# A planner's costs, its settings and its written order change in a fused attention and mixer block on one core

## Chip, core and metric

The kernel runs on one core of one Trainium2 chip. The metric is the device time of one execution in microseconds (us), the median of the runs taken. The trace comes from one profiled execution; its span runs from the first to the last instruction, and its device time is a little longer.

The engines are named as in the profile: PE is TensorE (PEld its weight loads), DVE VectorE, ACT ScalarE, POOL GpSimd, SP the queue that issues all DMAs. Each engine works through its own instructions strictly in the order in which they were put down.

## The reference, cut to what is computed

```python
# S = 2048 rows, D = 448, H = 16 heads of 28, W = 8 keys at distance 0, 2, ... 14; F = 1792
def _A_ref(x, wqkv, wo):
    q, k, v = split(x @ wqkv)
    idx = pos[:, None] - (arange(8) * 2)[None, :]          # masked where idx < 0
    logits = einsum("bhsd,bhswd->bhsw", q, k[idx]) * Dh ** -0.5
    return einsum("bhsw,bhswd->bhsd", softmax(logits), v[idx]) @ wo

def _B_ref(x, w1, w2, w3, w4):
    h = gelu(layernorm(x) @ w1)
    hs = concat(h quarters, moved by 1, -1, 2, -2 rows) @ w2
    x1 = x + hs
    return x1 + gelu(layernorm(x1) @ w3) @ w4

h  = x + _A_ref(layernorm(x), A_wqkv, A_wo)
h2 = h + _B_ref(layernorm(h), B_w1, B_w2, B_w3, B_w4)      # returned
```

## The kernel before

The 2048 rows are 16 tiles of 128 rows, handled in four blocks `t` of four tiles. The work of a block is cut into phases. `N1` normalizes the block's rows into the buffer `lntm` (mean and variance on DVE, the power -0.5 on POOL into `rs_y`, minus mean times that into `nmr`, then one pass for each tile on the engine that NORM names: `a` ACT, `v` DVE, `p` POOL). A small DVE `COPY lntm<-lntm` then repeats the last 64 columns of the block's four tiles at once. `A1` turns `lntm` into `actT` (TURN: `t` is 16 PE transposes and their eviction by ACT, `d` a DMA transpose that SP issues) and makes q, k and a joint rest `r` on PE: seven groups, whose accumulators (`ps`) ACT evicts into `arena`. `V` makes v, which ACT evicts into `vt` and DMAs spread into `vw`. `A2` makes the products of q with eight shifted k on DVE (`qk_r`, four instructions: three of 4096 columns and one of 2048), sums them on PE with a 0/1 matrix `zc`, and does the softmax (`mx`, `ls`, `zs`, `pb`), whose result PE transposes through `ident`. `A3` spreads the weights into a band on DVE (`bd_r`, a product with the mask `bmask`, four a block), multiplies with `vw` on PE, and then `wo_s` (the part `O`); the residual is added either on PE (the rows `ps<-xin,ident`) and evicted by ACT, or on DVE (RESIDUAL; PE too wherever the row sums are taken on the way). `B1` is the second normalization and `w1` (`ps<-actT,w_s`), `B2` the product with `w2` (`ps<-w_s,arena`) and the third normalization. From `B2` on the tiles form units `u` of 3, 4, 4, 4 and 1 tiles. `W3` makes the 14 groups of `h3T`, `B3` sums them with `w4` (`ps<-arena,h3T`), DVE adds and writes `ost`, and SP stores the rows. For the unit of one tile `phase_W3` calls no contraction, so no `W3` instruction of that unit stands in the program.

Nothing is placed by hand except the setup. All phases are recorded as operations with a duration in ns and their dependences, and `_Sched.schedule` plays them through: at each step it takes, among the engines' ready operations, the one that can start first, and within an engine prefers the one whose phase stands earlier in the string PLAN. Buffers and accumulator banks go round in the same way. The result is one fixed order for each engine and the semaphore waits between them. The durations, PLAN and the other settings (TURN, NORM, STATS, EVICT, RESIDUAL, LOADS, ROUNDS) therefore change the order of instructions everywhere. STATS names who takes the sums for a block's variance: `v` is DVE's BN_STATS and BN_AGGR, `a` is an ACT pass with a running sum. LOADS names the block behind whose `vw` DMAs the loads of w3 and w4 are issued.

In the recorded setup on POOL the mask `bmask` (a memset and eight affine selects) is made together with `zc` and others after the last normalization of block 0 (`setup`, `after=[last]`). All instructions carry the line 952, where the order is emitted; so the rows are told apart by tiles and by time.

Of the kernel before, what the change touches and what calls it, by code (L numbers as in the profile page):

```python
# [12 lines left out]
PLAN = "N1 0, A1 0, N1 1, T 0, A2 0, T 1, N1 2, A1 1, V 0, A2 1, S 0, N1 3, A3 0, O 3, M 1, A1 2, B1 0, S 1, O 1, V 1, A2 2, A3 1, B2 0, A1 3, S 2, M 0, V 2, B1 1, W3 0, A3 2, A2 3, O 2, B2 1, M 3, V 3, B1 2, S 3, W3 1, B2 2, W3 2, A3 3, B3 0, B1 3, B2 3, O 0, T 2, W3 3, B2 4, B3 1, W3 4, T 4, B3 2, T 3, B3 3, M 2, B3 4"  # L13
# [130 lines left out]
class _Sched:  # L144
# [66 lines left out]
    def schedule(self, dma_bw=190.0, dma_fixed=2000.0, table_load=1300.0):  # L211
# [22 lines left out]
        table = None  # L234
        for _ in range(n):
# [134 lines left out]
def bass_sequential_preLN__sliding_local_dilated__mixer_s_mlp__prompt_kernel(  # L370
# [32 lines left out]
    with ExitStack() as es:  # L403
# [74 lines left out]
        def dve(meth, n, mode=1.0, ns=None, **kw):  # L478
            return S.add("dve", meth, ns or (90 + n / mode) / 0.96, 205.0, **kw)
# [61 lines left out]
        def sums_stats(kind, tiles, src, ln):  # L541
            lo, m = tiles[0], len(tiles)
            dve("tensor_scalar", 4, ns=78.0, out=nm[:, kind, lo:lo + m], in0=mv[:, kind, lo:lo + m, 0], scalar1=-1.0 / D, scalar2=None, op0=ALU.mult)
            for n, i in enumerate(tiles):
                act(normalized(ln, n), src(i), ACT.Square, D, ns=655.0, bias=nm[:, kind, i:i + 1], accum_out=mv[:, kind, i, 1:2])

        def rstd(kind, i, m=4, summed=False, norm="v"):
# [3 lines left out]
            def power(k):  # L551
                S.add("pool", "tensor_tensor", (395.0 if m > 2 else 357.0) * m, 60.0, out=rs_y[:, kind, k, i:i + m], in0=rs_x[:, kind, k, i:i + m],
# [22 lines left out]
        def normalize(kind, i, out_ap, in_ap, summed=False, norm="v"):  # L575
# [3 lines left out]
            if norm == "p":  # L579
                return S.add("pool", "tensor_scalar", 1250.0, 60.0, out=out_ap, in0=in_ap, scalar1=nm[:, kind, i:i + 1] if summed else mv[:, kind, i, 0:1],  # L580
# [71 lines left out]
        def setup(after):  # L652
# [24 lines left out]
            later("memset", 154, ap=bmask[:], constant=0.0)  # L677
            for w in range(NW):
                later("affine_select", 200, out=bmask[:].rearrange("p (m e r) -> p m e r", m=4, e=2),
                      in_=bmask[:].rearrange("p (m e r) -> p m e r", m=4, e=2), pattern=[[16, 4], [1, 2], [DIL, NW]],  # L680
                      compare_op=ALU.not_equal, fill=1.0, base=PADK - DIL * w, channel_multiplier=-1)
# [75 lines left out]
        def phase_A2(t):  # L757
# [44 lines left out]
        def phase_A3(t):  # L802
            a = _Tile(P_act)
            sl = t % 2
            for il in range(4):
                bd = _Tile(P_bd)
                dve("tensor_tensor", 2048, ns=1136.0, out=bd(lambda v: v.rearrange("p (n g r) -> p n g r", g=8, r=NW)),
                    in0=pt[t][:, il * 256:il * 256 + 256].rearrange("p (n r) -> p n r", r=NW).unsqueeze(2).broadcast_to([KW, 32, 8, NW]),
                    in1=bmask[:].rearrange("p (g r) -> p g r", r=NW).unsqueeze(1).broadcast_to([KW, 32, 8, NW]), op=ALU.mult)
                b = _Tile(P_bank)  # L810
# [47 lines left out]
        def phase_B2(u):  # L858
            tiles = UNITS[u]
            summed = STATS["B2"][u] == "a"  # L860
            for i in tiles:
# [4 lines left out]
                dve("scalar_tensor_tensor", D, ns=740.0 if summed else 606.0, out=xb[i], in0=xin[:, i, :], scalar=rs_y[:, 1, 0, i:i + 1],  # L866
# [10 lines left out]
            for i in tiles:  # L877
                S.add("pool", "tensor_tensor", 1020.0, 100.0, after=nz, out=xb[i], in0=xb[i], in1=xin[:, i, :], op=ALU.add)
# [115 lines left out]
```

## Time and profile before

| what | value |
|---|---|
| median of 3 runs | 212.34 us (211.83 to 212.98) |
| the profiled execution | 212.65 us, its span 210.6 us |
| PE busy | 188.1 us, 89% of the span |
| DVE busy | 133.3 us, 63% |
| ACT busy | 108.9 us, 52% |
| POOL busy | 70.5 us, 33% |
| mean granted TensorE clock | 0.968 |

Rows of the timeline give start, duration, engine, operation, `out<-in`, the count of merged instructions, and in brackets the idle time of the engine ahead of the row with what ended it. "PE busy" is the union of matmul intervals; where PE has no bracket it did not wait.

### The profile page before, as it was taken

Reading aid. Unit: us, or ns where it says so; the run is one execution under the profiler, and the core shown is the slowest. Engines: PE = TensorE matmul, PEld = TensorE weight load, DVE = VectorE, ACT = ScalarE, POOL = GpSimd, SP = SyncE. Lnnn points to the kernel's source line nnn. Section 1 sums busy time; section 2 is a strip of 40 time slices with the busy share of each in tenths; the row PEclk is TensorE's granted clock in tenths of the full one; section 3 lists DMA queues with packets and bytes.
Section 4 is the critical chain, followed back from the end, with each engine's and each line's share of the span. In section 5 each row is a group of like instructions: output and inputs, shape, how many; then the busy total and the mean of one; then the engine's idle time right before and its main releaser. Section 6 shows DMA issues by size and latency. Waiting matters only on the chain.

```text
span 210.6 us, 3865 instructions
## 1 busy us (share of the span) xinstructions
PE 188.1 (89%) x1568; PEld 88.4 (42%) x1568; DVE 133.3 (63%) x253; ACT 108.9 (52%) x227; POOL 70.5 (33%) x93
## 2 busy tenths in 40 slices
PE   6797199989099977999799999999999999999994
PEld 2442043433044433544345544445544445534554
DVE  6459199994299998999994986549701626100222
ACT  3747554887157999854079265471035291057000
POOL 3488401499700520705714710004350015500000
PEclk9999859999769999999999999999999999999999
DMA  5677351990058577561304510000650002600111
GB/s 176 216 223 154 86 117 34 201 292 16 0 112 209 194 76 99 117 100 24 54 0 86 110 51 26 0 3 0 143 121 0 3 0 69 143 0 3 44 44 44
DMA packets 33137, 17.84 MB, mean 85 GB/s; under 512 B 21872, under 2 KB 32608, under 8 KB 33120
## 3 DMA queue, kind: packets, MB, share of 16 engines
q1 hardware_dynamic: 33120, 17.60, 36.7%
q8 instruction: 12, 0.20, 0.4%
q14 instruction: 5, 0.04, 0.1%
HBM read 7.91 MB, written 1.84 MB: 46 GB/s over the span
## 4 chain that ended last, share of the span: by engine, by line
PE 62%; POOL 15%; DVE 12%; ACT 6%; DMA 2%; issue 1%; POOLq 0%
PE ps L952 62%; POOL lntm L952 7%; DVE qk_r L952 3%; ACT lntm L952 3%; POOL bmask L952 3%; POOL rs_y L952 3%; DMA actT<-lntm 2%; DVE bd_r L952 2%; DVE lntm L952 2%; DVE st L952 2%; ACT actT L952 1%; DVE zs L952 1%; ACT arena L952 1%; POOL arena L952 1%; DVE pb L952 1%
## 5 line engine op out<-in xcount | busy, mean ns | idle before, releaser
L952 PE MATMUL ps<-actT,arena 128*128 128x512 bf16 (+4 forms) x348 | 68.6, 364 | 0.8 <-ACT arena L952 0.5
L952 POOL TENSOR_TENSOR rs_y<-rs_x,mhalf 128x4 f32<-128x4 f32 (+2 forms) x20 | 23.4, 1172 | 97.8 <-DVE rs_x L952 97.8
L952 ACT ACTIVATE arena<-ps 128x512 bf16<-128x512 f32 (+5 forms) x67 | 31.7, 531 | 24.8 <-PE ps L952 24.3
L952 PE MATMUL ps<-arena,h3T 128*128 128x448 bf16 (+1 forms) x238 | 44.0, 341 | 0.0
L952 ACT ACTIVATE h3T<-ps 128x512 bf16<-128x512 f32 (+1 forms) x56 | 27.6, 589 | 31.2 <-PE ps L952 31.2
L952 PEld LDWEIGHTS ps<-actT,arena 128*128 128x128 bf16 (+1 forms) x348 | 27.2, 97 | 35.7 <-issue 8.5
L952 DVE TENSOR_TENSOR qk_r<-arena 128x4096 bf16<-128x4096 bf16 (+1 forms) x16 | 33.4, 2111 | 2.0 <-ACT arena L952 1.8
L952 PEld LDWEIGHTS ps<-arena,h3T 128*128 128x128 bf16 x238 | 23.2, 98 | 19.3
L952 DVE SCALAR_TENSOR_TENSOR ost<-ps,mrs,arena 128x448 bf16<-128x448 f32 (+1 forms) x17 | 11.0, 654 | 29.8 <-PE ps L952 29.8
L952 POOL TENSOR_TENSOR arena<-arena,xin 128x448 f32<-128x448 f32 x16 | 19.7, 1258 | 8.4 <-DVE lntm L952 8.4
L952 DVE SCALAR_TENSOR_TENSOR arena<-xin,rs_y,ps 128x448 f32<-128x448 bf16 x16 | 10.4, 673 | 18.6 <-PE ps L952 18.4
L952 ACT ACTIVATE actT<-ps 128x512 bf16<-128x512 f32 (+2 forms) x22 | 13.8, 644 | 10.5 <-PE ps L952 10.5
L952 DVE TENSOR_TENSOR bd_r<-arena,bmask 80x2048 bf16<-80x2048 bf16 x16 | 18.8, 1214 | 0.6 <-ACT arena L952 0.6
L952 DVE BATCH_NORM_STATS2 st<-xin 128x6 f32<-128x448 bf16 x28 | 17.1, 609 | 1.1 <-DMA xin<-in_A_x_dram 1.1
L952 PE MATMUL ps<-arena,actT 128*128 128x448 bf16 (+1 forms) x64 | 14.5, 385 | 1.4 <-ACT actT L952 1.4
L952 PE MATMUL ps<-wo_s,actT 128*128 128x448 bf16 x64 | 15.0, 366 | 0.3 <-ACT actT L952 0.3
L952 PE MATMUL ps<-actT,w_s 128*112 128x512 bf16 (+1 forms) x64 | 14.1, 389 | 1.1 <-DMA actT<-lntm 1.1
L952 POOL TENSOR_SCALAR lntm<-xin,mv,rs_y 128x448 bf16<-128x448 bf16 x4 | 14.0, 3498 | 0.1
L952 PE MATMUL ps<-w_s,arena 112*128 112x448 bf16 x64 | 13.4, 353 | 0.1
L952 DVE COPY lntm<-lntm 128x256 bf16<-128x256 bf16 (+2 forms) x16 | 3.5, 218 | 15.0 <-ACT lntm L952 7.6
L952 ACT ACTIVATE lntm<-xin,nmr,rs_y 128x448 bf16<-128x448 bf16 x12 | 8.5, 751 | 7.1 <-POOL nmr L952 7.1
L952 PE MATMUL ps<-bd_r,vw 80*32 80x64 bf16 x512 | 6.9, 200 | 5.6 <-DVE bd_r L952 5.6
(63 smaller groups left out, 157.9 us busy)
## 6 DMA issues: line engine op xcount, KB each, us to landing
out_dram<-ost SPq DMA_DIRECT2D x15, 112.0 KB, 1.7
arena<-in_B_w_dram SPq DMA_DIRECT2D x1, 1568.0 KB, 10.1
arena<-in_B_w_dram SPq DMA_DIRECT2D x1, 1344.0 KB, 9.8
vw<-vt SPq DMA_DIRECT2D x4, 320.0 KB, 4.6
vw<-vt SPq DMA_DIRECT2D x4, 256.0 KB, 4.2
xin<-in_A_x_dram SPq DMA_DIRECT2D x2, 448.0 KB, 10.6
xin<-in_A_x_dram SPq DMA_DIRECT2D x3, 224.0 KB, 4.5
arena<-in_A_wqkv_dram SPq DMA_DIRECT2D x1, 672.0 KB, 4.4
```

Source lines behind the costliest of these rows:

```text
L952: inst = getattr(eng, meth)(**kw)
```

## The change

Six things are edited, and the schedule that comes out of them differs on every engine:

1. `schedule` knows a flag `block`. It is set on DVE's `qk_r` and `bd_r` products and on POOL's residual additions (`arena<-arena,xin`). In the playing through, a POOL operation now starts no earlier than the end of the last flagged DVE product, and a flagged DVE product no earlier than the end of a flagged POOL addition. It adds no wait to the program; it only changes where the planner puts operations.
2. Costs that the planner uses: the power on four columns is 250 ns a column in place of 395, a sum-taking DVE addition 615 in place of 740 ns, a POOL normalization 1780 in place of 1250.
3. No normalization is left on POOL (block 3 of `N1` goes to DVE), and that block's sums are taken on ACT (a Copy pass and a Square pass).
4. `bmask` is made directly after the first constants, ahead of the powers of block 0.
5. `A1` turns all four blocks on PE, `B2` its first unit; in blocks 2 and 3 DVE evicts three of `A1`'s seven groups; unit 1 of `W3` has two rounds in place of three; w3 is loaded behind block 1 like w4.
6. PLAN and the other settings are new.

```diff
-PLAN = "N1 0, A1 0, N1 1, T 0, A2 0, T 1, N1 2, A1 1, V 0, A2 1, S 0, ...
+PLAN = "S 1, N1 0, M 2, N1 1, A1 0, V 0, A2 0, A3 0, A1 1, O 0, V 1, ...
-TURN = {'A1': 'ttdd', 'B1': 'dddd', 'B2': 'ddddd'}
-NORM = {'N1': 'aavp', 'B1': 'avvv', 'B2': 'vvvva'}
-STATS = {'B1': 'avvv', 'B2': 'aavav'}
-EVICT = 'aaaa'
+TURN = {'A1': 'tttt', 'B1': 'dddd', 'B2': 'tdddd'}
+NORM = {'N1': 'aavv', 'B1': 'avva', 'B2': 'avava'}
+STATS = {'N1': 'vvva', 'B1': 'avav', 'B2': 'avvvv'}
+EVICT = 'aavv'
...
-LOADS = '21'
-RESIDUAL = 'ttvv'
+RUNS = {'A3': '1111', 'W3': '32334'}
+LOADS = '11'
+RESIDUAL = 'tvvv'
...
+        blocked = held = 0.0
...
+                if op.eng == "pool":
+                    st = max(st, blocked)
+                    if op.block:
+                        held = st + dur
+                elif op.block:
+                    st = max(st, held)
+                    blocked = st + dur
...
-                S.add("pool", "tensor_tensor", (395.0 if m > 2 else 357.0) * m, 60.0, ...
+                S.add("pool", "tensor_tensor", (250.0 * m if m > 2 else 355.0 * m), 60.0, ...
...
-            later("memset", 154, ap=bmask[:], constant=0.0)
-            for w in range(NW):
-                later("affine_select", 200, out=bmask[:] ...
...
+                    if summed:
+                        act(normalized(ln, i % 4), xin[:, i, :], ACT.Copy, D, ns=655.0, accum_out=mv[:, 0, i, 0:1])
...
         warm()
         pads()
+        S.add("pool", "memset", 154, 60.0, ap=bmask[:], constant=0.0)
+        for w in range(NW):
+            S.add("pool", "affine_select", 275, 60.0, out=bmask[:] ...
```

Three places of the new order follow, each as it stands before and after.

POOL, from the setup to the fourth block's normalization, before (`ls` and `arena` memsets stand ahead of it):

```order
L952 MEMSET arena 64x16
L952 MEMSET bmask 80x64
L952 AFFINE_SELECT bmask<-bmask 80x64 x8
L952 MEMSET vw 16x512
L952 TENSOR_TENSOR rs_y<-rs_x,mhalf 128x4
L952 TENSOR_TENSOR nmr<-nm,rs_y 128x4
L952 TENSOR_TENSOR rs_y<-rs_x,mhalf 128x4 x2
L952 TENSOR_SCALAR lntm<-xin,mv,rs_y 128x448 x4
```

The start of POOL after:

```order
L973 MEMSET mhalf 128x8
L973 MEMSET arena 112x4x2 x2
L973 MEMSET bmask 80x64
L973 AFFINE_SELECT bmask<-bmask 80x64 x8
L973 TENSOR_TENSOR rs_y<-rs_x,mhalf 128x1
L973 TENSOR_TENSOR nmr<-nm,rs_y 128x1
```

And the same stretch of POOL as above, after:

```order
L973 MEMSET arena 64x16
L973 MEMSET vw 16x512
L973 TENSOR_TENSOR rs_y<-rs_x,mhalf 128x4
L973 TENSOR_TENSOR nmr<-nm,rs_y 128x4
L973 TENSOR_TENSOR rs_y<-rs_x,mhalf 128x4 x3
L973 TENSOR_TENSOR nmr<-nm,rs_y 128x4
```

The nine mask instructions stand ahead of the first powers, the `vw` memset and block 1's power follow the setup directly, and the four normalizations are gone.

ACT, from the eviction of block 0's `A1` to the turn of block 1, before:

```order
L952 ACTIVATE arena<-ps 128x512 x6
L952 ACTIVATE arena<-ps 64x256 x3
L952 ACTIVATE arena<-ps 64x272
L952 ACTIVATE arena<-ps 64x16
L952 ACTIVATE arena<-arena 128x3x16
L952 ACTIVATE vt<-ps 128x16x28 x2
L952 ACTIVATE lntm<-xin,nmr,rs_y 128x448 x4
L952 ACTIVATE vt<-ps 128x16x28 x2
L952 ACTIVATE actT<-ps 128x1024 x2
```

and after:

```order
L973 ACTIVATE arena<-ps 128x512 x5
L973 ACTIVATE lntm<-xin,nmr,rs_y 128x448 x4
L973 ACTIVATE arena<-ps 128x512
L973 ACTIVATE arena<-ps 64x256 x3
L973 ACTIVATE arena<-ps 64x272
L973 ACTIVATE arena<-ps 64x16
L973 ACTIVATE arena<-arena 128x3x16
L973 ACTIVATE vt<-ps 128x16x28 x4
L973 ACTIVATE actT<-ps 128x1024 x2
```

Block 1's four normalizations move up into the middle of the evictions, ahead of the last `arena` and all `vt` rows.

DVE, from the products of block 1 to the first bands, before (the `COPY` is block 3's, behind its POOL normalization):

```order
L952 TENSOR_SCALAR rs_x<-mv 128x4
L952 TENSOR_TENSOR qk_r<-arena 128x4096 x2
L952 TENSOR_TENSOR bd_r<-arena,bmask 80x2048 x2
L952 TENSOR_TENSOR qk_r<-arena 128x4096
L952 TENSOR_TENSOR qk_r<-arena 128x2048
L952 COPY lntm<-lntm 128x4x64
L952 TENSOR_TENSOR bd_r<-arena,bmask 80x2048 x2
```

and after:

```order
L973 TENSOR_SCALAR rs_x<-mv 128x4
L973 TENSOR_REDUCE mx<-ps 128x64
L973 TENSOR_TENSOR ls<-ps,mx 128x512
L973 TENSOR_SCALAR lntm<-xin,nm,rs_y 128x448 x3
L973 TENSOR_TENSOR bd_r<-arena,bmask 80x2048
L973 TENSOR_REDUCE zs<-ls 128x64
L973 RECIPROCAL zs<-zs 128x64
L973 TENSOR_TENSOR pb<-ls,zs 128x8x64
L973 TENSOR_TENSOR bd_r<-arena,bmask 80x2048 x3
L973 CAST arena<-ps 128x512 x3
L973 TENSOR_SCALAR lntm<-xin,nm,rs_y 128x448
L973 COPY lntm<-lntm 128x4x64
```

Block 3's normalization is now on DVE itself, its power is asked for behind a softmax row and not a product, and the `COPY` no longer has POOL ahead of it.

More of the change, by code (lines that the diff above doesn't have):

```diff
@@ L551, in power @@
             def power(k):
-                S.add("pool", "tensor_tensor", (395.0 if m > 2 else 357.0) * m, 60.0, out=rs_y[:, kind, k, i:i + m], in0=rs_x[:, kind, k, i:i + m],
+                S.add("pool", "tensor_tensor", (250.0 * m if m > 2 else 355.0 * m), 60.0, out=rs_y[:, kind, k, i:i + m], in0=rs_x[:, kind, k, i:i + m],
                       in1=mhalf[:, 0:m], op=ALU.pow)
@@ L804, in phase_A3 @@
             sl = t % 2
[L805 to L810, printed above, removed]
+            width = int(RUNS["A3"][t])
+            for first in range(0, 4, width):
+                made = []
+                for il in range(first, first + width):
+                    bd = _Tile(P_bd)
+                    dve("tensor_tensor", 2048, ns=1136.0, block=True, out=bd(lambda v: v.rearrange("p (n g r) -> p n g r", g=8, r=NW)),
+                        in0=pt[t][:, il * 256:il * 256 + 256].rearrange("p (n r) -> p n r", r=NW).unsqueeze(2).broadcast_to([KW, 32, 8, NW]),
+                        in1=bmask[:].rearrange("p (g r) -> p g r", r=NW).unsqueeze(1).broadcast_to([KW, 32, 8, NW]), op=ALU.mult)
+                    made.append((il, bd, _Tile(P_bank)))
                 mms([(b(lambda v, j=j, lo=128 * c + 64 * a2: v[32 * j:32 * j + 32, lo:lo + 64]),
@@ L813, in phase_A3 @@
                       bd(lambda v, lo=(16 * a2 + 4 * c + j) * 64: v[:, lo:lo + 64]), True, True, 64, j)
-                     for c in range(4) for a2 in range(2) for j in range(4)])
-                act(a(lambda v, il=il: v[:, il, :, :].rearrange("p c n -> p (c n)").rearrange("p (m r e) -> p m r e", r=NW, e=2)),
-                    b(lambda v: v.rearrange("p (m e r) -> p m r e", r=NW, e=2)), ACT.Copy, 512)
+                     for il, bd, b in made for c in range(4) for a2 in range(2) for j in range(4)])
+                for il, bd, b in made:
+                    act(a(lambda v, il=il: v[:, il, :, :].rearrange("p c n -> p (c n)").rearrange("p (m r e) -> p m r e", r=NW, e=2)),
+                        b(lambda v: v.rearrange("p (m e r) -> p m r e", r=NW, e=2)), ACT.Copy, 512)
             part("O", t)
@@ L865, in phase_B2 @@
                 kw = dict(accum_out=mv[:, 2, i, 0:1]) if summed else {}
-                dve("scalar_tensor_tensor", D, ns=740.0 if summed else 606.0, out=xb[i], in0=xin[:, i, :], scalar=rs_y[:, 1, 0, i:i + 1],
+                dve("scalar_tensor_tensor", D, ns=615.0 if summed else 606.0, out=xb[i], in0=xin[:, i, :], scalar=rs_y[:, 1, 0, i:i + 1],
                     in1=b(lambda v: v[:, 0:D]), op0=ALU.mult, op1=ALU.add, **kw)
@@ L877, in phase_B2 @@
             for i in tiles:
-                S.add("pool", "tensor_tensor", 1020.0, 100.0, after=nz, out=xb[i], in0=xb[i], in1=xin[:, i, :], op=ALU.add)
+                S.add("pool", "tensor_tensor", 1020.0, 100.0, after=nz, out=xb[i], in0=xb[i], in1=xin[:, i, :], op=ALU.add).block = True
             b2_a[u] = transposed(ln, TURN["B2"][u], len(tiles))
@@ L893, in group @@
                         lambda: act(h3[u][f](lambda v: v[:, 0:128 * n]), b(lambda v: v[:, 0:128 * n]), ACT.Gelu_apprx_tanh, 128 * n), h3[u][f])
-            h3_last[u] = [contract([group(f) for f in range(NF)], ROUNDS["W3"] if n > 1 else ROUNDS["W3 1"])] if n > 1 else []
+            h3_last[u] = [contract([group(f) for f in range(NF)], ROUNDS["W3"][RUNS["W3"][u]])] if n > 1 else []
         def phase_B3(u):
```

38 lines of the change are left out of this document (22 added, 16 removed).

## Prediction

> **What bounds the kernel now.** I read the page's header and clock row first, then PE's own timeline for its idle times, then for each long one the engine named in its bracket and back from there, and last the windows, for what PE idles in each half of the run.
>
> ```profile
> span 210.6 us, 3865 instructions
> PEclk9999859999769999999999999999999999999999
> 14.07:83.99 69.92, 54.87 (x591) 23.58 (x590) 55.03 (x74) 48.98 (x109) 30.70 (x28) 0.90 0.57 127
> 83.99:207.90 123.91, 122.45 (x918) 59.31 (x918) 69.14 (x149) 53.67 (x110) 32.41 (x31) 1.00 0.24 50
> ```
>
> The two windows (stretch, length, then busy PE, PEld, DVE, ACT, POOL, clock) split the run where the first `w1` matmul starts, at 83.99. Behind it PE idles 123.91 - 122.45 = 1.5 us: that stretch is PE work and nothing else. Ahead of it PE idles 69.92 - 54.87 = 15.1 us, and the clock is 0.90. So only the first 84 us have anything to give.
>
> ```profile
> 20.76 1.05 PE L952 MATMUL ps<-qk_r,zc 128*32 128x512 bf16 x16 [1.39 <-DVE qk_r L952]
> 26.52 1.89 PE L952 MATMUL ps<-ident,lntm 128*128 128x128 bf16 x16 [4.72 <-DVE lntm L952]
> 28.68 2.42 PE L952 MATMUL ps<-arena,actT 128*128 128x448 bf16 x6 [0.26 <-ACT actT L952]
> 58.24 0.62 PE L952 MATMUL ps<-bd_r,vw 80*32 80x64 bf16 x32 [5.63 <-DVE bd_r L952]
> 60.57 1.61 PE L952 MATMUL ps<-wo_s,actT 128*128 128x448 bf16 x4
> 62.20 0.92 PE L952 MATMUL ps<-wo_s,actT 128*128 128x448 bf16 x4
> 71.21 0.42 PE L952 MATMUL ps<-bd_r,vw 80*32 80x64 bf16 x32
> 79.63 1.31 PE L952 MATMUL ps<-arena,actT 128*128 128x448 bf16 x6
> 83.99 3.50 PE L952 MATMUL ps<-actT,w_s 128*112 128x512 bf16 x16 [0.97 <-DMA actT<-lntm]
> 24.50:31.20 6.70, 4.41 (x26) 2.48 (x30) 4.89 (x8) 4.50 (x7) 0.00 (x0) 0.50 0.40 85
> 55.30:61.80 6.50, 3.56 (x71) 1.76 (x72) 4.94 (x6) 1.72 (x4) 1.49 (x1) 0.50 0.43 83
> ```
>
> Two waits, 4.72 and 5.63 us, are 10.35 of the 15.1. Each also brings half the clock for some 6.7 us (the two windows at 0.50), which starts some 2.6 us into the idle time. Six `arena,actT` matmuls take 2.42 us there and 1.31 later, four `wo_s` 1.61 against 0.92, a row of 32 band matmuls 0.62 against 0.42. In the first slow stretch lie those six (1.1), sixteen turns (1.89 against 1.5, by the row of eight further down: 0.4) and a product row (0.1): 1.6 us lost. In the second lie two band rows (0.4), four `wo_s` (0.7) and three `arena,actT` (half of 1.1): 1.7. The wait of 1.39 brought no half clock.
>
> Who makes PE wait:
>
> ```profile
> 14.58 7.14 POOL L952 TENSOR_SCALAR_AFFINE_SELECT bmask<-bmask 80x64 bf16<-80x64 bf16 x8
> 22.16 1.02 POOL L952 TENSOR_TENSOR rs_y<-rs_x,mhalf 128x4 f32<-128x4 f32 x1
> 23.26 0.20 POOL L952 TENSOR_TENSOR nmr<-nm,rs_y 128x4 f32<-128x4 f32 x1
> L952 POOL TENSOR_SCALAR_AFFINE_SELECT bmask<-bmask x8: 290/293/2281, 14.6 to 21.4; 80x64 bf16<-80x64 bf16 x8
> L952 POOL MEMSET bmask<- x1: 176/176/176, 14.3 to 14.3; 80x64 bf16 x1
> 39.59 3.15 POOL L952 TENSOR_TENSOR rs_y<-rs_x,mhalf 128x4 f32<-128x4 f32 x1 [6.94 <-DVE rs_x L952]
> L952 POOL TENSOR_SCALAR lntm<-xin,mv,rs_y x4: 1858/1858/8416, 42.8 to 54.9; 128x448 bf16<-128x448 bf16 x4
> 16.17 4.53 DVE L952 TENSOR_TENSOR qk_r<-arena 128x4096 bf16<-128x4096 bf16 x2 [1.82 <-ACT arena L952]
> 39.58 4.49 DVE L952 TENSOR_TENSOR qk_r<-arena 128x4096 bf16<-128x4096 bf16 x2
> 43.99 2.35 DVE L952 TENSOR_TENSOR bd_r<-arena,bmask 80x2048 bf16<-80x2048 bf16 x2
> 46.26 3.41 DVE L952 TENSOR_TENSOR qk_r<-arena 128x4096 bf16<-128x4096 bf16 x2
> 56.83 0.23 DVE L952 COPY lntm<-lntm 128x256 bf16<-128x256 bf16 x1 [7.15 <-POOL lntm L952]
> 14.07 4.70 ACT L952 ACTIVATE arena<-ps 128x512 bf16<-128x512 f32 x11 [2.54 <-PE ps L952]
> 18.93 0.98 ACT L952 ACTIVATE vt<-ps 128x448 bf16<-128x448 f32 x2
> 23.49 2.71 ACT L952 ACTIVATE lntm<-xin,nmr,rs_y 128x448 bf16<-128x448 bf16 x4 [3.58 <-POOL nmr L952]
> 27.60 1.94 ACT L952 ACTIVATE actT<-ps 128x1024 bf16<-128x1024 bf16 x2 [0.54 <-PE ps L952]
> ```
>
> Two forms of row stand here: the timeline's, and a tile's (durations in ns: least, median, most; first and last start). First wait: block 1's power stands behind the mask on POOL. A select takes 0.29 us, but up to 2.28 when a product of DVE runs, and two were caught so; the mask lasts to 21.7, and ACT normalizes block 1 from 23.49. Second wait: POOL's first normalization takes 8.416 us against 1.858 for its fellows: it does not move until DVE's products end at 49.67. Block 3 is done at 56.8, and the `COPY` that waits for it holds the whole DVE for 7.15 us, the bands of block 0 behind it, and so PE.
>
> **The change, part by part.** All against the profiled span of 210.6.
>
> *No normalization on POOL, and the order of POOL against products: -7.3.* Block 3's normalization becomes four DVE passes, three behind a softmax row, the last with the `COPY` behind the bands; POOL has only one power of 1.0 us ahead of them, asked for while DVE has no product. The second wait goes with its slow clock: 5.63 + 1.7. What is late next is PE's turn of block 3, which needs that `COPY`: behind the first band stand three more (1.2 each), a softmax's end (1.9) and three CASTs (0.6, by the xin row below), which puts it at 53.6 in my walk. Three `wo_s` groups stand ahead of it on PE and are through at 54.5, so it costs nothing; without that cover it would be 1 to 2 us. The other end, that POOL's powers cost as much under products as now (3.15), is the first rival.
>
> *The mask first: -6.3, and +0.3.* Without the mask (14.3 on), and with the `vw` memset (22.16 - 21.7, 0.45) behind the setup, block 1's power starts at 14.7 in place of 22.16 and its `nmr` ends near 16.0, ahead of the product at 16.17. So the wait of 4.72 and its 1.6 of slow clock go; what takes their place is two parts further down. The mask now runs at the start: 7.14 less the two caught selects' 3.8 is 3.3, with memset and gaps 3.7, from 1.7 to 5.4, and it holds the first power:
>
> ```profile
> 4.04 0.56 POOL L952 TENSOR_TENSOR rs_y<-rs_x,mhalf 128x1 f32<-128x1 f32 x1 [2.38 <-DVE rs_x L952]
> 7.11 0.74 PE L952 MATMUL ps<-ident,lntm 128*128 128x128 bf16 x8
> 1.53 0.14 POOL L952 MEMSET arena<- 112x8 bf16 x2
> 4.69 0.19 POOL L952 TENSOR_TENSOR nmr<-nm,rs_y 128x1 f32<-128x1 f32 x1
> 9.28 0.76 ACT L952 ACTIVATE lntm<-xin,nmr,rs_y 128x448 bf16<-128x448 bf16 x1
> L952 DVE TENSOR_TENSOR xin<-ps,xin 128x448 bf16<-128x448 f32 x8 | 4.8, 618 | 0.6 <-PE ps L952 0.3
> ```
>
> That power starts 1.4 later, but ACT's last of the four normalizations stood at 9.28 behind evictions that wait for PE's opening matmuls; four pairs of power and `nmr` (0.84, with gaps 0.95) from 5.4 and the evictions between them bring it to 9.6. Later by 0.3, with everything behind; bounds 0 and 1.4.
>
> *ACT's new order: +2.3.* After five evictions (0.49 each, 14.4 to 16.9) come block 1's normalizations (2.7, to 19.5), then the other evictions (2.4) and four `vt` (1.9, to 23.6), and only then the two `actT` of 1.94: to 25.5. PE meanwhile ends `V` at 19.7 (20.76 - 1.39, and 0.3), waits for the `COPY` behind two products (21.1), turns, sums a product, is through at 23.4 and waits for `actT` to 25.5. So 1.5 + 2.1 idle in place of 1.39. Bounds: nothing, if ACT gets through as fast as PE, and +1.6 more, if 2.1 us idle halve the clock as 4.72 did; 1.39 did not, and 2.1 lies nearer to that, so I take none. The Trainium skill ("TensorE: Matmul & The Clock Gate", What's actually happening) has the clock halved after an idle window of some 3.4 us whose phase is free-running. By that rule 2.1 us would cost nothing; the trace shows half clock 2.6 us after idling began, so the measurement is the sharper bound.
>
> *More turns on PE: +4.1.* `A1` turns two more blocks (32 matmuls) and `B2` its first unit (12). Eight took 0.74: 44 x 0.093 = 4.1, on PE, which is the bound from then on. The three DMA turns that go bring nothing by themselves: PE waited for turns 0.97 and, in one more row, 0.17 us. ACT gets five more evictions of `actT`; DVE takes six of ACT's (CAST), so ACT's load to the first `w1` rises from 49.0 by 3.9 (four `actT` pieces of 0.97), 5.4 (block 3's sums, eight passes at the 0.68 of 23.49), less 2.9 (six evictions of 0.49) and 2.1 (four residuals): 53.3 us. That is 88% of the time it is given below.
>
> *Other waits ahead of `w1`: -0.6.* The first window's remaining idle time is 15.1 - 10.35 - 1.39 = 3.3, with the 0.97 at 83.99. Walking the new orders with these durations I find waits of 1.15 (second `wo_s`, for its `actT` behind `r`'s evictions), 0.45, 0.3, 0.2 and some tenths: 2.7. My walk passes `A1` of block 1 at 25.6, of block 2 at 42.7, of block 3 from 61 on, and reaches `w1` at 73.8; the DMA turn it needs, 4.9 behind a `COPY` at 68.4, is there at 73.3. Bounds: -2 and, if that turn takes the 7.9 of now (76.12 to 83.99), +2.5.
>
> *Behind `w1`: +1.2.* Idle 1.5 before. New: 0.4 for the first band of block 2, 0.25 for the gelu, and the DMA turn of the second `B1`:
>
> ```profile
> 76.12 4.48 SPq L952 DMA_TRANSPOSE actT<-lntm  x1
> 88.65 4.86 DMA actT<-lntm
> arena<-in_B_w_dram SPq DMA_DIRECT2D x1, 1568.0 KB, 10.1
> ```
>
> 4.86 us behind a `COPY` that ends 3.2 us ahead of PE's last other work: 1.7 idle, and 0.4 near the last `W3`. In all 2.7. At worst that turn takes 7.9 as well: +3; at best it is hidden: -1.7. The loads of w3 and w4 (10 us each) now run one behind the other near 41 to 61, ahead of those turns; the `vw` of block 2 waits for them and for `A3` of block 0 (near 54), and is needed near 77. The residuals' places, unit 1's two rounds and LOADS itself: nothing, on PE the matmuls are the same.
>
> How much POOL holds up DVE in turn: the two products of 39.58 take 4.49 with a power beside them that ends 0.9 us into the second, those of 16.17 take 4.53 with two selects. So nothing; the other end is one power each, four ahead of `w1` at 1.0: +4. The Trainium skill ("SBUF — State Buffer", Who interferes with whom) says that the two engines share a port pair, which the first instruction holds to its end while the other blocks fully. The 8.416 agrees; by that rule the second product should have waited, and 4.49 shows that it did not.
>
> Sum: -7.3 - 6.3 + 0.3 + 2.3 + 4.1 - 0.6 + 1.2 = -6.3. Span 204.3; with the 2.05 around it (212.65 - 210.6) 206.3; the profiled run lies 0.3 over the median of 212.34, so **206.0**.
>
> **Rivals.** *POOL is caught all the same.* `nmr` of block 1 ends only some 0.2 us ahead of the first product. Caught, it waits one product (2.27), ACT's normalizations stand in its queue ahead of everything, PE idles 4.4 in one piece and the clock halves: 2.3 + 1.6 = 3.9, so 209.9. For it: two selects were caught at just that product. Against: both paths start from the same last normalization and shift together. *DVE waits for POOL's powers*: +4, 210, if each holds a product to its end; against it stands the 4.49. That is the port rule of the page named above.
>
> *ACT becomes the gate: slower.* Ahead of `w1` ACT was busy 48.98 of 69.92, 70%. All evictions, sums and turns now pass it in one order. If it stays no denser, 53.3 us of work need 76.1: `w1` starts at 14.4 + 76.1 = 90.5, 6.5 later than now, and with 1.1 for unit 0's turn the time is 212.3 + 7.6 = 219.9. It decides from the point where ACT idles over 15 us there (`w1` past 83). For it: ACT has no slack from 14.4 to 25.5. Against: 10.35 of its 20.9 idle were the two waits for POOL; with only these gone, `w1` starts at 78.3 and the time is 208; the walk gives 73.8.
>
> *The gain is moved, not made.* If the DMA turns take 7.9 (+3) and `nmr` is caught (+3.9), 206.0 + 6.9 = 212.9: no change.
>
> **How the numbers follow.** Forecast 78%, `nmr` caught 8%, products behind powers 3%, ACT the gate 6%, given back 5%. The range reaches from 202.5 (new waits of 2.3 and 1.2 not there) to 210 (a caught `nmr`); the clock's +1.6 and a slow turn's +3 lie inside. Half a per cent, 1.1 us, is about what this measurement can tell from nothing. Faster holds the first three but for 0.01 of a forecast that falls short, 0.88; same the last one and that 0.01, 0.06; slower ACT's 0.06.
>
> **What would show it.** PE: no wait over 3 us before `w1`, the clock row at 9 from the second slice on, `w1` near 74, some 2 us idle ahead of block 1's `A1`, released by ACT. POOL: selects all near 0.3 us, `nmr` of block 1 done before the first product. DVE: no wait for POOL of 7 us. PE busy about 188.1 - 3.3 + 4.1 = 189. Wrong if the clock row dips again, if ACT is the releaser of PE for more than 6 us before `w1`, or if DMA turns take 8 us.

## The result, and the profile after

The changed kernel took 204.62 us (median of four runs, 203.40 to 205.55) against 212.63 for the one before (also four runs): a ratio of 0.9625, 95% interval 0.9564 to 0.9686. The forecast was 206.0. The profiled execution took 204.91 us, with a span of 202.9. The times given further down leave out four slow executions: of the kernel with the mask late again a profiled one of 250.49 us, at a mean clock of 0.752, and two of 213.04 and 213.52 at 0.968, and of the one planned without the flag a profiled one of 378.99, whose 128x512 matmuls took 668 ns where another execution of it had 390.

The header, the engines' busy time and the clock row of the page after, and two windows that meet where the first `w1` matmul starts:

```profile
span 202.9 us, 3968 instructions
PE 187.6 (92%) x1612; PEld 90.4 (45%) x1612; DVE 132.4 (65%) x244; ACT 120.9 (60%) x250; POOL 52.5 (26%) x92
PEclk9879999999999999999999999999999999999999
26.68:73.09 46.41, 44.61 (x561) 20.32 (x561) 44.11 (x58) 40.58 (x96) 6.35 (x6) 1.00 0.51 130
73.09:200.20 127.11, 123.95 (x935) 60.79 (x934) 70.01 (x142) 62.94 (x124) 33.34 (x34) 1.00 0.20 45
```

Both dips of the clock in the middle are gone; a small one (the 8 and the 7) stands near the start. `w1` begins at 73.09 in place of 83.99. Ahead of it PE now idles 73.09 - (187.6 - 123.95) = 9.4 us, before 83.99 - (188.1 - 122.45) = 18.3; behind it 3.2 in place of 1.5. So 10.9 us were won ahead of `w1`, and 3.2 given back behind it (127.11 against 123.91; 1.7 of it is idle time and 1.5 more work of PE): 7.7 in all.

PE's timeline after, the rows at the places that the prediction named, and two that it did not (92.44, and the nine at half speed at 9.76):

```profile
9.76 2.13 PE L973 MATMUL ps<-actT,arena 128*128 128x256 bf16 x9
13.00 4.50 PE L973 MATMUL ps<-actT,arena 128*128 128x256 bf16 x28 [0.20 <-ACT actT L973]
22.27 1.07 PE L973 MATMUL ps<-ident,lntm 128*128 128x128 bf16 x16 [1.49 <-DVE lntm L973]
26.68 3.73 PE L973 MATMUL ps<-actT,arena 128*128 128x512 bf16 x19 [2.37 <-ACT actT L973]
52.67 0.93 PE L973 MATMUL ps<-wo_s,actT 128*128 128x448 bf16 x4 [1.08 <-ACT actT L973]
83.80 1.50 PE L973 MATMUL ps<-actT,w_s 128*112 128x512 bf16 x6 [1.01 <-DMA actT<-lntm]
92.44 0.84 PE L973 MATMUL ps<-ident,lntm 128*128 128x128 bf16 x12 [1.38 <-DVE lntm L973]
```

POOL's timeline after, at the start, at block 1's power, and at unit 0's third normalization:

```profile
1.90 3.33 POOL L973 TENSOR_SCALAR_AFFINE_SELECT bmask<-bmask 80x64 bf16<-80x64 bf16 x8
5.20 0.56 POOL L973 TENSOR_TENSOR rs_y<-rs_x,mhalf 128x1 f32<-128x1 f32 x1
14.92 1.01 POOL L973 TENSOR_TENSOR rs_y<-rs_x,mhalf 128x4 f32<-128x4 f32 x1
16.01 0.20 POOL L973 TENSOR_TENSOR nmr<-nm,rs_y 128x4 f32<-128x4 f32 x1
85.99 4.04 POOL L973 TENSOR_TENSOR nmr<-nm,rs_y 128x3 f32<-128x3 f32 x1
```

Block 1's `nmr` is through at 16.2, 1.4 us ahead of the first product (17.58, below). The last row is an operation that takes 0.20 us at 16.01: it was caught by the two products that start at 85.49, and ends at 90.03, just behind the end of the second (89.97).

The products of both places, and what waits behind that `nmr`:

```profile
17.58 4.49 DVE L973 TENSOR_TENSOR qk_r<-arena 128x4096 bf16<-128x4096 bf16 x2 [3.12 <-ACT arena L973]
85.49 4.48 DVE L973 TENSOR_TENSOR qk_r<-arena 128x4096 bf16<-128x4096 bf16 x2
90.06 2.06 ACT L973 ACTIVATE lntm<-arena,nmr,rs_y 128x448 bf16<-128x448 f32 x3 [1.74 <-POOL nmr L973]
92.16 0.23 DVE L973 COPY lntm<-lntm 128x192 bf16<-128x192 bf16 x1 [2.19 <-ACT lntm L973]
```

### The profile page after: what moved, and what is told of

It reads as the page before. It is cut to its first block, busy times and chain, and to the rows that moved or that the text cites. A ratio compares the mean times of both kernels' runs of the same rounds, so it can differ in the third digit from the quotient of the medians.

```text
span 202.9 us, 3968 instructions
## 1 busy us (share of the span) xinstructions
PE 187.6 (92%) x1612; PEld 90.4 (45%) x1612; DVE 132.4 (65%) x244; ACT 120.9 (60%) x250; POOL 52.5 (26%) x92
## 4 chain that ended last, share of the span: by engine, by line
PE 64%; DVE 16%; ACT 12%; POOL 5%; issue 1%; POOLq 0%
PE ps L973 64%; DVE qk_r L973 4%; ACT arena L973 4%; DVE bd_r L973 3%; ACT lntm L973 3%; ACT actT L973 3%; POOL nmr L973 2%; DVE arena L973 1%; POOL bmask L973 1%; DVE xin L973 1%; DVE zs L973 1%; DVE lntm L973 1%; DVE st L973 1%; POOL rs_y L973 1%; ACT vt L973 1%
## 5 line engine op out<-in xcount | busy, mean ns | idle before, releaser
L973 PE MATMUL ps<-actT,arena 128*128 128x512 bf16 (+4 forms) x348 | 70.4, 369 | 2.6 <-ACT actT L973 2.6
L973 POOL TENSOR_TENSOR rs_y<-rs_x,mhalf 128x4 f32<-128x4 f32 (+2 forms) x20 | 21.2, 1064 | 101.5 <-DVE rs_x L973 101.5
L973 ACT ACTIVATE arena<-ps 128x512 bf16<-128x512 f32 (+5 forms) x61 | 28.9, 524 | 14.0 <-PE ps L973 13.5
L973 ACT ACTIVATE actT<-ps 128x512 bf16<-128x512 f32 (+2 forms) x28 | 19.4, 715 | 4.5 <-PE ps L973 4.4
L973 POOL TENSOR_TENSOR arena<-arena,xin 128x448 f32<-128x448 f32 x16 | 16.2, 1040 | 10.8 <-ACT lntm L973 5.9
L973 ACT ACTIVATE lntm<-xin,nmr,rs_y 128x448 bf16<-128x448 bf16 x16 | 11.2, 760 | 10.8 <-POOL nmr L973 10.8
L973 DVE SCALAR_TENSOR_TENSOR arena<-xin,rs_y,ps 128x448 f32<-128x448 bf16 x16 | 10.5, 663 | 3.9 <-PE ps L973 3.9
L973 DVE BATCH_NORM_STATS2 st<-xin 128x6 f32<-128x448 bf16 x20 | 12.1, 607 | 1.0 <-DMA xin<-in_A_x_dram 1.0
L973 PE MATMUL ps<-arena,actT 128*128 128x448 bf16 (+1 forms) x64 | 12.4, 354 | 0.4 <-ACT actT L973 0.3
L973 PE MATMUL ps<-ident,lntm 128*128 128x128 bf16 x76 | 6.4, 229 | 4.9 <-DVE lntm L973 4.9
L973 DVE TENSOR_TENSOR xin<-ps,xin 128x448 bf16<-128x448 f32 x8 | 5.0, 623 | 8.0 <-PE ps L973 7.8
```

Source lines behind the costliest of these rows:

```text
L973: inst = getattr(eng, meth)(**kw)
```

## The experiments

Each kernel below is the one before or after with its planner's result edited: operations are moved within the engines' lists, and all others keep their places. Only the runs without the flag and with DMA turns are planned anew. The edits are shown abridged, without helper functions and definitions. Times are medians, ratios are to the kernel before on the same chip. Differences to the changed kernel are to its 204.62, from another set of runs; the kernel before lay between 212.63 and 213.00 in these sets. First come edits of the changed kernel that undo or alter one thing, then edits of the kernel before that do one thing alone.

**The mask late again.** The nine mask instructions go back to directly ahead of the `vw` memset.

```diff
         order = S.schedule()
+        mask_ = [op for op in order["pool"] if _writes(op, "bmask")]
+        _move(order["pool"], mask_, next(op for op in order["pool"] if _writes(op, "vw")))
```

> The changed kernel with every engine's order kept, only the nine mask instructions on POOL put back between the setup and the vw memset. Theory (the mask in front of block 1's power makes the first long wait): POOL's power of block 1 starts near 22 instead of 14.9, and since ACT now has block 1's normalizations ahead of its last evictions, A1 of block 1 starts near 32 instead of 26.7, with half the clock for a window; the opening gets 1.1 us back. Together +6 to +7 us over the changed kernel, 211. Rival (the new order alone hides the mask): +0 to +2, 205 to 207.

209.8 us, ratio 0.9871 (0.9827 to 0.9915): 5.2 above the changed kernel, by three runs at a clock of 0.982 or 0.983; the two of 213.04 and 213.52 lie 3.5 higher still. POOL and PE in its only trace, which is that of the 250.49 us:

```profile
14.29 7.22 POOL L1007 TENSOR_SCALAR_AFFINE_SELECT bmask<-bmask 80x64 bf16<-80x64 bf16 x8
21.95 1.02 POOL L1007 TENSOR_TENSOR rs_y<-rs_x,mhalf 128x4 f32<-128x4 f32 x1
26.30 1.89 PE L1007 MATMUL ps<-ident,lntm 128*128 128x128 bf16 x16 [4.98 <-DVE lntm L1007]
```

The wait of before (4.72) is back, released by the same `COPY`, and would be longer at full clock: the 28 matmuls of block 0's `A1` took 5.61 us here and 4.50 in the changed kernel. By the times the mask's place is worth 5 us or more in the new order too, which rules out that the new order hides the mask.

**The mask behind block 1's `nmr`.** Neither the start nor block 1's power waits for it then.

```diff
+        nmr_ = [op for op in order["pool"] if _writes(op, "nmr")][4]
+        _move(order["pool"], mask_, order["pool"][order["pool"].index(nmr_) + 1])
```

> The changed kernel, only the mask moved on POOL to directly behind the nmr of block 1, into a stretch where POOL idles 9 us. Theory (the mask in front of the first powers costs the opening 1.4 us, and nothing needs the mask before 45): the 28 A1 matmuls of block 0 start near 11.6 to 11.9 instead of 13.0, no half clock near 10 us, two or three selects are caught by products (2.2 us each) and nobody waits for them: -1.1 to -1.4 us, 203.3. Rival (the slow window near 10 us is the clock's own phase and not the mask's doing): within 0.3 us of the changed kernel.

203.78 us, ratio 0.9581 (0.9536 to 0.9626), 0.8 below the changed kernel; the intervals overlap, but the spans of the runs at 0.999 or 1.000 (201.1 to 201.3 against 201.7) say 0.4 to 0.6 as well. The turns of block 1 start 1.5 us earlier, and all of that is lost again in the profiled run, whose first `w1` stands at 73.08:

```profile
20.79 1.07 PE L1008 MATMUL ps<-ident,lntm 128*128 128x128 bf16 x16 [1.63 <-DVE lntm L1008]
25.05 5.37 PE L1008 MATMUL ps<-actT,arena 128*128 128x512 bf16 x19 [2.22 <-ACT actT L1008]
```

After a wait of 2.22 the 19 matmuls took 5.37; after one of 2.37 in the changed kernel's profile they took 3.73. The same program ran in 202.83, 202.84 and 203.06 at a mean clock of 0.999 or 1.000, and in 204.51, 204.64 and 204.91 at 0.992. So one window of half clock costs 1.6 us by the row and 1.8 by the two groups' means, and whether it comes differs from run to run. That it stands behind this wait is seen in the profiled run (204.64) alone.

**Block 1's turn ahead of the `vt` rows.** ACT's two `actT` evictions move ahead of the four `vt`.

```diff
+        turn_ = [op for op in order["act"] if _writes(op, "actT")][4:6]
+        _move(order["act"], turn_, next(op for op in order["act"] if _writes(op, "vt")))
```

> The changed kernel, only ACT's two actT evictions of block 1's turn put ahead of the four vt evictions. Theory (PE's wait of 2.4 us ahead of A1 of block 1 is ACT's queue and nothing else): A1 of block 1 starts near 24.9 instead of 26.7, -1.7 us, 202.9, if nothing behind it is late. Rival (the accumulator banks that the vt rows free are what A1 needs next, or the vw DMAs come late): PE waits as long a little later, 204.5 to 205.

203.29 us, ratio 0.9547 (0.9511 to 0.9583), 1.3 below the changed kernel; the intervals just overlap, but the spans at equal clock (200.3 against 201.7 at 1.000) say 1.4. PE's wait of 2.37 is 0.61, and two waits for DVE's products are new or longer (0.22 before the second of them in the changed kernel):

```profile
24.90 3.73 PE L1007 MATMUL ps<-actT,arena 128*128 128x512 bf16 x19 [0.61 <-ACT actT L1007]
35.99 1.05 PE L1007 MATMUL ps<-qk_r,zc 128*32 128x512 bf16 x16 [0.43 <-DVE qk_r L1007]
40.58 1.05 PE L1007 MATMUL ps<-qk_r,zc 128*32 128x512 bf16 x16 [0.56 <-DVE qk_r L1007]
```

The later rows come 1.33 us earlier (75.55 against 76.88 for block 2's first band): 1.8 won, 0.5 given back to DVE.

**Block 3's normalization on POOL again**, behind its power.

```diff
+        norm_ = [op for op in dve_ if op.insts[0][0] == "tensor_scalar" and _writes(op, "lntm")][4:8]
+        for op in norm_:
+            dve_.remove(op); op.eng = "pool"
+        pool_[power_ + 1:power_ + 1] = norm_
```

> The changed kernel, only block 3's four normalizations moved from DVE to POOL, behind their power. Theory (what POOL loses to DVE's products depends on how many of them run meanwhile; here three bands and no product): the four take 7.1 us of their own and stand still during the bands, so the COPY comes near 56 instead of 53.9, PE's turn of block 3 about 1.3 later: +1 to +2 us, 206. Rival (a normalization on POOL costs the whole second wait of before wherever it stands): +6 to +7 us, 211.

205.04 us, ratio 0.9638 (0.9587 to 0.9689): no difference from the changed kernel. The tile's group in its trace (least, median, most ns):

```profile
L1010 POOL TENSOR_SCALAR lntm<-xin,nm,rs_y x4: 708/714/1675, 45.3 to 48.4; 128x448 bf16<-128x448 bf16 x4
```

They were through at 49.1, long ahead of the `COPY` at 54.8, since only one band runs beside them. So it is not the engine that cost 7 us before, but POOL's turn falling under two pairs of products and the bands between them (39.58 to 49.67). And a pass took 0.71 us, where before it took 1.86. The next run asks why.

**The same with subtract.**

```diff
+            op.insts[0][1]["op0"] = ALU.subtract
```

> The changed kernel with block 3's four normalizations back on POOL, behind their power, and with subtract in place of add as the first of the two operations, all operands the same; so these rows get x plus the mean, and the computation differs there. It asks why POOL's pass took 1.86 us in the kernel before and 0.71 us in the run with add. Theory (the operation sets it): 1.86 us each, done near 52.8, ahead of the COPY near 54, and no change of time, 204 to 206. Rival (the operand, or DVE's work beside it, set it): 0.7 us each, and the same time.

205.86 us, ratio 0.9638 (0.9577 to 0.9699).

```profile
L1011 POOL TENSOR_SCALAR lntm<-xin,nm,rs_y x4: 1854/2064/4022, 45.3 to 53.4; 128x448 bf16<-128x448 bf16 x4
```

The operation sets it: 1.85 at least with subtract, 0.71 with add, all operands the same. With four bands beside them they end at 55.2, and the `COPY` waited 0.15 for them, so the old operation costs nothing at this place either.

**Planned without the flag.**

```diff
-                if op.eng == "pool":
+                if False:
...
-                elif op.block:
+                elif False:
```

> The changed kernel planned without the flag: a POOL operation may start under a DVE product in the planner's play, and a product under an addition. The plan differs in 23 rows of DVE, 8 of ACT and 16 of PE. Theory (with no normalization on POOL and the mask first, little is left on POOL that a product could catch): 204 to 206, within 1 us of the changed kernel. Rival (the flag itself keeps POOL and DVE apart and holds part of the gain): powers caught by products, 207 or more.

Five runs of 209.62 to 212.02, ratio 0.9899 (0.9856 to 0.9942): 5.7 above the changed kernel, and the theory fell. At an equal clock, 0.991 or 0.992, it is about 4.7 (209.62 to 210.35 against 204.91 and 205.55). The rows come from one more execution:

> The same kernel as the one planned without the flag, for a profile: in the first one the matmuls ran at half speed from end to end, so it shows no waits. Its plan differs from the changed kernel's only behind block 2's bands: PE sums block 3's products in two parts around w3's first group, ACT's normalization of unit 0 stands ahead of the gelu evictions, and DVE makes all of block 3's products ahead of unit 0's sums. Theory (POOL's small nmr and additions of unit 0 now run under DVE's products): rows ahead of w1 (near 73) stand as in the changed kernel, and PE has 4 to 6 us more idle between 80 and 125, behind a COPY or an addition that POOL held up. Rival: the loss lies ahead of w1, or in ACT's order with no POOL row caught.

210.2 us. A window, and rows of PE, POOL, ACT and DVE in that trace:

```profile
73.10:130.00 56.90, 50.70 (x474) 24.64 (x473) 43.20 (x74) 34.90 (x74) 22.18 (x16) 0.97 0.25 46
73.53 3.47 PE L973 MATMUL ps<-actT,w_s 128*112 128x512 bf16 x16
87.42 4.04 POOL L973 TENSOR_TENSOR nmr<-nm,rs_y 128x3 f32<-128x3 f32 x1
93.63 6.05 POOL L973 TENSOR_TENSOR arena<-arena,xin 128x448 f32<-128x448 f32 x3 [2.17 <-ACT lntm L973]
91.49 2.06 ACT L973 ACTIVATE lntm<-arena,nmr,rs_y 128x448 bf16<-128x448 f32 x3 [3.89 <-POOL nmr L973]
93.73 5.07 DVE L973 TENSOR_TENSOR qk_r<-arena 128x4096 bf16<-128x4096 bf16 x2
103.38 7.21 PE L973 MATMUL ps<-actT,arena 64*128 64x384 bf16 x47 [1.19 <-DVE arena L973]
111.11 3.50 PE L973 MATMUL ps<-actT,w_s 128*112 128x512 bf16 x16 [0.33 <-DMA actT<-lntm]
```

and the additions and the `w1` of block 2 in the changed kernel:

```profile
92.20 3.04 POOL L973 TENSOR_TENSOR arena<-arena,xin 128x448 f32<-128x448 f32 x3 [2.18 <-ACT lntm L973]
105.97 3.46 PE L973 MATMUL ps<-actT,w_s 128*112 128x512 bf16 x16
```

The first `w1` stands at 73.53, as in the changed kernel (73.09). The loss is behind it: from there to the `w1` of block 2 it is 37.58 us in place of 32.88, 4.7 more. Unit 0's three additions start together with block 3's products and take 6.05, twice as long; DVE's sums for unit 0 wait behind these products. ACT's gelu evictions now stand behind the normalization that the caught `nmr` holds, and ACT idles 3.89 where it idled 1.74. The `nmr` itself is caught for 4.04 in both kernels. PE's idle time from 73.1 to 130 is 6.2 in place of 3.1, and a stretch of half clock is in it again (mean clock 0.97 in place of 1.00). The shares of the additions and of ACT's order weren't taken apart.

**`A1`'s blocks 2 and 3 turned by DMA**, planned anew.

```diff
-TURN = {'A1': 'tttt', 'B1': 'dddd', 'B2': 'tdddd'}
+TURN = {'A1': 'ttdd', 'B1': 'dddd', 'B2': 'tdddd'}
```

> The changed kernel planned with A1's blocks 2 and 3 turned by DMA as before, and planned anew, so that rows of all engines move a little. Theory (PE is the bound, and 32 turns at 0.067 us are on it): about 2 us less PE work, 202 to 203.5. Rival (a DMA turn takes 4.9 us and its latency stands on the path of two blocks): new waits of PE of 1 us and more, 204.6 or more.

213.55 us, ratio 1.0047 (1.0017 to 1.0076), 9 above the changed kernel. SP's queue and PE there:

```profile
46.36 14.15 SPq L973 DMA_DIRECT2D vw<-vt  x4
60.62 5.94 SPq L973 DMA_TRANSPOSE actT<-lntm  x1
58.16 1.05 PE L973 MATMUL ps<-qk_r,zc 128*32 128x512 bf16 x16 [1.32 <-DVE qk_r L973]
61.78 0.62 PE L973 MATMUL ps<-bd_r,vw 80*32 80x64 bf16 x32 [2.57 <-DVE bd_r L973]
69.81 0.42 PE L973 MATMUL ps<-bd_r,vw 80*32 80x64 bf16 x32 [2.23 <-DVE bd_r L973]
```

The planner put block 3's normalization behind two more products, its turn is issued only at 60.6 and takes 5.94, and until 66.6 PE has no `A1` of block 3 to work on while it waits for DVE. The turns and the order changed together here, so the run gives no price of a turn. It shows how far one setting moves a plan.

**The kernel before, block 3's normalization on DVE ahead of the `COPY`**, and nothing else.

```diff
+        norm_ = [op for op in pool_ if _writes(op, "lntm")]
+        for op in norm_:
+            pool_.remove(op); op.eng = "dve"
+        dve_[dve_.index(copy_):dve_.index(copy_)] = norm_
```

> The kernel before with one edit: block 3's four normalizations stand on DVE, directly ahead of the COPY, in place of POOL; every other instruction keeps its place. Theory (the second wait was POOL held off by DVE's products, and is lost from the end): DVE reaches the COPY at about 51 in place of 56.83, PE's wait of 5.63 and its slow clock go, and the time falls by 5 to 7 us, to 206 to 208. Rival (the order behind is tight as well, and the wait comes back at another product): a fall of under 2.5 us, 210 or more.

206.61 us, ratio 0.9697 (0.9675 to 0.9719): -6.4.

```profile
49.34 1.30 DVE L990 TENSOR_SCALAR lntm<-xin,mv,rs_y 128x448 bf16<-128x448 bf16 x4
50.67 0.23 DVE L990 COPY lntm<-lntm 128x256 bf16<-128x256 bf16 x1
52.28 0.42 PE L990 MATMUL ps<-bd_r,vw 80*32 80x64 bf16 x32
```

The `COPY` comes 6.2 earlier and PE's wait of 5.63 is gone.

**The kernel before, the mask first**, ahead of block 0's powers. The mask's dependence on block 0's last normalization, which the recorded setup gave it, is dropped with it.

```diff
+        _move(order["pool"], mask_, next(op for op in order["pool"] if _writes(op, "rs_y")))
```

> The kernel before with one edit: the nine mask instructions stand ahead of block 0's first powers on POOL. Theory (the first wait was block 1's power behind the mask): ACT normalizes block 1 from its last vt row ahead of it, at about 19.9 in place of 23.49, so PE's wait of 4.72 falls to about 1 and its slow clock goes (-3.6 - 1.6), while the start is later by 0.3 to 1.4: 208 to 209. Rival (the block 1 turn is held by something else, the COPY behind DVE's products): the wait keeps over 3 us, and the time falls by under 2 us, to 211 or more.

210.0 us, ratio 0.9864 (0.9829 to 0.9899): -3.0, between the two expectations.

```profile
12.97 4.50 PE L988 MATMUL ps<-actT,arena 128*128 128x256 bf16 x28 [0.17 <-ACT actT L988]
24.21 1.07 PE L988 MATMUL ps<-ident,lntm 128*128 128x128 bf16 x16 [1.05 <-DVE lntm L988]
55.51 0.62 PE L988 MATMUL ps<-bd_r,vw 80*32 80x64 bf16 x32 [5.62 <-DVE bd_r L988]
```

The wait of 4.72 is 1.05 (with 0.67 and 1.08 new behind it), as the theory had it; the start is 1.4 later, with a window of half clock in it. The other wait stands as it was.

**The kernel before with both edits, the mask behind block 1's `nmr`.**

> The kernel before with two edits and no new order: block 3's normalizations on DVE ahead of the COPY, and the mask on POOL directly behind block 1's nmr. No start is delayed. Theory (the two POOL waits are the whole of the gain, and the searched order adds nothing to it): -5 to -7 for the one and -5 for the other, 201 to 203, at or below the changed kernel's 204.6. Rival (the new order of all engines is needed to keep the gain): 205.5 or more.

202.49 us (202.04 to 202.62), ratio 0.9503 (0.9481 to 0.9525): -10.5. Its clock row, the largest wait between the opening and `w1`, and `w1`:

```profile
PEclk9999999999999999999999999999999999999999
20.58 1.05 PE L994 MATMUL ps<-qk_r,zc 128*32 128x512 bf16 x16 [1.39 <-DVE qk_r L994]
73.85 3.50 PE L994 MATMUL ps<-actT,w_s 128*112 128x512 bf16 x16 [1.23 <-DMA actT<-lntm]
```

Two moved pieces of work in the old order, with the old turns, beat the whole change (204.62). The mask stands later here than in the changed kernel, which was worth 0.8 of these 2.1 us there; what else the change does cost about 1.3 us more than it brought.

**The changed kernel with both of its opening edits**, the mask behind block 1's `nmr` and block 1's turn ahead of `vt`.

> The changed kernel with the mask moved behind block 1's nmr and block 1's two actT evictions moved ahead of the vt rows on ACT. Theory (the two opening costs are separate, 1.4 at the start and 1.7 ahead of block 1's A1): both go, and with no wait over 1.5 us left there no window of half clock follows: 201 to 202.5, level with the kernel before plus its two edits (202.5). Rival (what the opening gains is given back to DVE's products of block 0 and 1): 203 or more.

202.11 us (201.59 to 202.94), ratio 0.9506 (0.9473 to 0.9539): level with the run above, 2.5 below the changed kernel, and below either kernel of this case. All six runs had a clock of 1.000. The two gains (0.8 and 1.3 alone) add up, and a little more: at 1.000 the spans, 199.8 to 200.4 against 201.7, give 1.3 to 1.9, and the rest is half clock, which two of the changed kernel's four runs had and none of these.

## Why the prediction was nearly right

**No normalization on POOL, -7.3.** Alone it is -6.4. The mechanism is shown: POOL's passes lost their time to products, the `COPY` inherited it, and with the passes elsewhere no wait takes its place. That POOL may keep them where only bands run (205.04, and 205.86 with the old subtraction) was not seen: what the term pays for is the place and not the engine.

**The mask first, -6.3 and +0.3.** Undone it costs 5.2 or more. The first part held. The start was mis-sized: 13.00 in place of 11.59 is +1.4. PE's group of these matmuls, before and after:

```profile
L952 PE MATMUL ps<-actT,arena 128*128 128x256 bf16 x24 | 3.1, 273 | 0.4 <-ACT actT L952 0.4
L973 PE MATMUL ps<-actT,arena 128*128 128x256 bf16 x24 | 4.3, 339 | 0.2 <-ACT actT L973 0.2
```

1.2 of the 1.4 is a window of half clock among PE's short opening waits (0.51, 0.55 and 0.93). The profile without the flag, with the same order there and waits of 0.71, 0.55 and 0.92, had none and began at 11.74: +0.15, as predicted. The upper bound of 1.4 had the right size by another mechanism.

**ACT's new order, +2.3.** The walk had waits of 1.5 and 2.1 at 21.1 and 25.5; they are 1.49 and 2.37 at 22.27 and 26.68, the second released by `actT`. (1.5 + 2.1 - 1.39 is 2.2 and not the 2.3 of the sum; measured it is 2.5.) That 2.1 does not halve the clock was half right: in the changed kernel's profile it did not, in five others with a wait of 2.22 to 2.37 there it did (5.37 to 5.42 for the 19 matmuls). The Trainium skill ("TensorE: Matmul & The Clock Gate", What's actually happening) has the window free-running, and this spread agrees; that it takes an idle window of some 3.4 us does not follow from these rows, where a wait of 2.22 was followed by half clock. In all six profiles a wait of 1.49 or 1.63 stands some 2 us ahead of it; where the second wait is cut to 0.61, in two profiles above, the first alone brought none. Half clock is a part of the spread of the measured time: 203.40 and 204.32 came at 1.000, each with a span of 201.7, 204.91 and 205.55 at 0.992 and 0.991, with 202.9 and 203.8. In the profiled one of them (204.91) the window is the opening's and not this wait's.

**44 more turns, +4.1.** PE's groups before and after:

```profile
L952 PE MATMUL ps<-ident,lntm 128*128 128x128 bf16 x32 | 3.4, 272 | 6.0 <-DVE lntm L952 6.0
L973 PE MATMUL ps<-ident,lntm 128*128 128x128 bf16 x76 | 6.4, 229 | 4.9 <-DVE lntm L973 4.9
```

The groups differ by 3.0, but in that are the old turns too, sixteen of which took 1.89 at half clock and now 1.07. The five new rows take 3.3: four of eight at 0.61 each and one of twelve at 0.84. The row that priced them, eight in 0.74 at 7.11, was a slow one: at the same place eight took 0.61 in the kernel before with block 3's normalization on DVE. That made the sum 0.8 us too long.

**Other waits ahead of `w1`, -0.6.** From 26.68 to 73.09 PE idled 46.41 - 44.61 = 1.8, with the largest wait 1.08 at the second `wo_s` as foreseen (1.15). The terms ahead of `w1` (32 of the turns among them) add up to -8.6 and would put it at 75.4, while the walk said 73.8; the prediction did not notice. It is 73.09: the walk, which also sees which work moves past a station, was the better of the two. Of the 2.3 by which the sum fell short here, 0.5 is the price of the 32 turns, and about 0.7 is work that moved behind `w1`, where PE was busy for 1.5 longer and the twelve turns are 0.84 of that; the rest isn't taken apart.

**Behind `w1`, +1.2.** It is 1.7: 0.32, 0.36 and 1.01 for the band, the gelu and the DMA turn (0.4, 0.25 and 1.7 foreseen), no wait near the last `W3`, and 1.38 that was not seen. That one is the first rival, *POOL is caught all the same*, at another place: not block 1's `nmr`, which had 1.4 us to spare where the walk gave it 0.2, but unit 0's, caught for 4.04 under the products of 85.49. ACT's normalization waits 1.74 for it, the `COPY` 2.19, PE 1.38.

**The rivals.** DVE's products did not wait for POOL's powers: the pair at 25.26, beside one of 2.99, took 3.42 (3.43 without one, at 38.41), the pair at 85.49 took 4.48 (4.49 at 17.58). ACT did not become the gate, though it is the releaser of the longest wait ahead of `w1`. The gain was not moved away, but a quarter of the 10.5 us that two edits are worth in the old order was.

**What it left out.** The prediction gave the flag no term of its own, since it acts only through the plan. The run without it shows that the flag is worth 4.7 to 5.7 us of that plan, nearly all of it behind the first `w1`, so not by the mask or block 3's normalization. It keeps unit 0's additions from block 3's products, and the order of ACT changes with it; which of the two is worth how much stays open. The Trainium skill ("SBUF — State Buffer", Who interferes with whom) says that a VectorE operation with two inputs in SBUF contends with a GpSimd operation that reads SBUF, and calls the port pair that they share an exclusive lock. The `nmr` of 4.04 agrees that it was shut out, but it was held to the end of the second product, past the end of the first.

**Its signs, and the total.** `w1` near 74, no wait over 3 us ahead of it, some 2 us idle ahead of block 1's `A1`, and selects of 0.29 came as written. One sign of being wrong came too: the clock row dips again, to 8 and 7 at the start, where the prediction had no window of half clock. The total is 1.4 off because the terms gave 2.3 too little ahead of `w1` (-8.6, measured -10.9) and 0.9 too little loss behind it (+1.2 and 1.1 for unit 0's turns, measured +3.2). That these two cancel in part is luck; the two large terms and their causes are not.

## What to carry to other kernels

When a large change of a plan gains, do its two or three nameable edits by hand in the old order before crediting the search: here two moves, one of them to a later place than the change chose, gave 10.5 us where the whole change gave 8.0. Look at GpSimd's smallest operations for durations far above their usual ones, and ask who is queued behind them: a 0.2 us multiply that takes 4 us can hold three engines in turn. Keep waits of TensorE short, and apart from one another: the one of 2.2 to 2.4 us ahead of block 1's `A1` was followed by half clock in five of six profiles, and three of 0.5 to 0.9 us in a row at the start were in some. Measure over several runs, because the clock is lost in some and not in others.

## What the runs showed of the hardware

A GpSimd pass over 128x448 bf16 with two scalars a row took 0.71 us with add and multiply, and 1.85 with subtract and multiply, the operands being the same. A GpSimd multiply of 0.20 us that began 0.5 us into the first of two VectorE products took 4.04, to the end of the second. Behind a wait of TensorE of 2.2 to 2.4 us at one place the clock was halved in five profiles and not in a sixth; a window of it costs 1.2 to 1.8 us here, so that runs of some kernels fall on steps (202.05 and 203.3; 203.34, 204.58 and 206.1) that the mean clock names: 1.000, 0.99 and 0.983. It does not name all of the spread: six runs at 1.000 lay between 201.59 and 202.94, and one at 0.991 was the fastest of its five (202.04).
